# Moving dWq and WK2 blocks in the order of TensorE's work, and transposing Y and KV earlier, in the backward pass of a linear-attention and SwiGLU block

## The chip, the cores and the metric

The kernel runs on one core of a Trainium2 chip. The metric is the device time of one execution in microseconds; three runs of the kernel before gave 814.64, 814.79 and 814.91 us, so the median is 814.79 us.

Five engines work beside each other: TensorE (PE in the profile, with its weight loads as PEld) multiplies matrices into PSUM; VectorE (DVE), ScalarE (ACT) and GpSimd (POOL) do elementwise work; SyncE (SP) here only starts DMAs. In this kernel SP starts every transposing DMA, and POOL most of the plain loads and stores.

## The reference, cut to what matters

The block is a layer norm, linear attention with 32 heads of 20 columns, a residual, a second layer norm, a SwiGLU FFN and a second residual. The kernel returns the output and the gradients of the input and of the five weights, with S = 2048 rows, D = 640 and F = 1728, in bf16.

```python
def _A_ref(x, wqkv, wo):                      # x is the normalised input
    qkv = (x @ wqkv).reshape(B, S, 3, H, Dh).transpose(2, 0, 3, 1, 4)
    q, k, v = qkv[0], qkv[1], qkv[2]
    phi = lambda t: jnp.where(t > 0, t + 1, jnp.exp(t)) + 1e-6
    pq, pk = phi(q), phi(k)
    kv = jnp.einsum("bhsd,bhse->bhde", pk, v)
    z = jnp.einsum("bhsd->bhd", pk)
    num = jnp.einsum("bhqd,bhde->bhqe", pq, kv)
    den = jnp.einsum("bhqd,bhd->bhq", pq, z)[..., None] + 1e-6
    return (num / den).transpose(0, 2, 1, 3).reshape(B, S, D) @ wo
...
h = x + _A_ref(_layernorm(x), A_wqkv, A_wo)
h2 = h + _B_ref(_layernorm(h), B_w_gate, B_w_up, B_w_down)     # _B_ref: (silu(x@wg) * (x@wu)) @ wd
# outputs: h2, and the vjp of grad_out for x, wqkv, wo, w_gate, w_up, w_down
```

The kernel never forms v. It forms Y = xn^T pk (640x640) and from it, head by head, KV; in the backward pass it forms GT = dh1^T pqs and from it dKV. The names that this text uses: dWq and dWk are the gradients of the q and k parts of wqkv (`dwqk`), dWv that of the v part (`dwv`, from Y and dKV), dWo that of wo (`dwo`, from KV and G, the transpose of GT). WK2 is a 640x640 product of the v weights with dKV, and WV2 its transpose.

## The kernel before: the parts that the change touches

The program runs in this order: layer norm and k, q; Y and KV; the attention output; four FFN groups of 448 columns (384 in the last), each with its forward and backward products and weight gradients; the loop for dhn and dq; and the last third, with dk, dxn, and finally the FFN output `ps_o`.

Some parts of the program have their order fixed as written (`manual_schedule` names the engines); for the others the order of an engine's instructions is chosen when the program is built.

Y^T and KV^T are written to DRAM early:

```python
nc.sync.dma_start(out=mat_v(scr_Yt), in_=Yt)
...
nc.sync.dma_start(out=scr_KVT.rearrange("(j p) c -> p j c", p=P), in_=KVT)
```

In the FFN (SP's order is fixed, the others' is not) each pair of rows is transposed through one of three `stg` buffers to DRAM. The dwev tiles, which carry weight gradients out of PSUM, share six buffers with nsg, u and a:

```python
def stage():
    return small.tile([P, 7, P], BF16, name="stg", tag="stg", bufs=3)
...
fpool = wB.enter_context(tc.tile_pool(name="fpool", bufs=6))       # nsg, u, a, dwev
...
for g in range(4):
    for t in range(0, ST, 2):
        ...                                                        # pg, pu: matmuls into PSUM
        sig = nc.scalar.activation(out=dg, in_=pg[:, :, :w], func=ACT.Sigmoid)
        nc.scalar.activation(out=nsg, in_=pg[:, :, :w], func=ACT.Sigmoid, scale=-1.0)
        nc.scalar.copy(out=m, in_=pg[:, :, :w])
        nc.scalar.copy(out=u, in_=pu[:, :, :w])
        ...                                                        # seven products on DVE
        for c in range(2):
            stg = stage()
            nc.sync.dma_start_transpose(out=stg[:, :GK[g], :], in_=ddt[:, tt + c, 0:2 * w])
            nc.gpsimd.dma_start(out=scr_dT[t + c, :, KO[g]:KO[g] + GK[g], :], in_=stg[:, :GK[g], :])
    if g == 0:
        wdT = strips.tile([P, DT, 2 * GM], BF16, name="wdT", tag="S")
        load_wdT(wdT, 2)
    ...
    # then the weight gradients: eight dw() per group, each ending in
    ev = fw("dwev")
    last = copy(out=ev[:, :len(parts), :w], in_=ps[:, :len(parts), :w])
    for c, (_, _, dst) in enumerate(parts):
        nc.gpsimd.dma_start(out=dst[:, GO[g]:GO[g] + w], in_=ev[:, c, :w])
```

The last third, in which the order of SP and DVE is fixed. GT, woT and W2T lie in one tile, `mats`, and the later matrices take their places:

```python
W2T = mat(0, DT, D); woT = mat(DT * D, DT, D)                      # from the loop before
...
load_pk(0); load_pk(1)                                             # the first two pkr loads
...                                                                # SP: 16 transposes into wqkvT
GT = mat(2 * DT * D, DT, D)
for i in range(DT): ...                                            # ps_gt, copied by ACT into GT
dKVT = mat(0, HG, P)
KV = mat(HG * P, HG, P)
G = mat(2 * HG * P, HG, D)
Y = mat(2 * HG * P + HG * D, HG, D)
nc.gpsimd.dma_start(out=mat_v(scr_GT), in_=GT)
...
def load_pqT(v):                                                   # two transposes into ring
    nc.sync.dma_start_transpose(out=ring[:, 4 + v % 3], in_=scr_pk[v * P:(v + 1) * P, :])
    nc.sync.dma_start_transpose(out=ring[:, 7 + v % 3], in_=dq[v // 8][:, v % 8, :])

def wk2(i):
    ps = mm("ps_wk2")
    mm_heads(ps, lambda j: wqkvT[:, 10 + j, i * P:(i + 1) * P], lambda j, a, b: dKVT[:, j, a:b])
    nc.scalar.copy(out=half(WK2[:, i, :]), in_=row(ps))
    nc.sync.dma_start_transpose(out=WV2[:, :, i * P:(i + 1) * P], in_=WK2[:, i, :])

def dwqk(which, i):
    ev = wk("dwqk", pool=i % 2)
    ps = mm("ps_dwqk")                                             # 2 halves of 320 columns, 16 matmuls each
    ...
    nc.scalar.copy(out=half(ev[:]), in_=row(ps))
    nc.gpsimd.dma_start(out=out_2[i * P:(i + 1) * P, which * D:(which + 1) * D], in_=ev[:])

for v in range(3):
    load_pqT(v)
for t in range(ST):
    nc.vector.tensor_scalar(out=xn_r[:, t, :], ...)                # normalise x again
dz_add(ZL, ztmp)                                                   # two DVE operations each
kv_blocks(dKVT, "ps_dkvt", ...)                                    # dKV from woT and GT
for t in range(ZL + 1, ST):
    dz_add(t, ztmp)
...                                                                # dzs, two DVE operations
dwqk(0, 0)
for i in range(3):
    wk2(i)
dwqk(0, 1)
for i in range(3, DT):
    wk2(i)
dwqk(0, 2)
...                                                                # ps_dzb from dzs
for t in range(ST + LAG):                                          # LAG = 3
    if t in (2, 3):
        dwqk(0, t + 1)
    if t < ST:
        if t + 2 < ST:
            load_pk(t + 2)
        ...                                                        # ps_dk, then dk[:, t] on DVE
        nc.sync.dma_start_transpose(out=ring[:, t % 4], in_=dk[:, t, :])      # dkT
    if 8 <= t < 8 + HG:
        tr_cols(G[:, t - 8, :], scr_GT, OH[t - 8])
    if t == 14:
        nc.sync.dma_start_transpose(out=KV.rearrange("p j c -> p (j c)").unsqueeze(1), in_=scr_KVT)
    ...
    ps = mm("ps_dxn")                                              # u = t - 3: from dqT, pkT with WV2, dkT
    ...
for t in range(ST):                                                # the FFN output
    if t + MTA < ST:
        load_mT(t + MTA)                                           # a transpose into mT
    if t < 3:
        for j in (2 * t, 2 * t + 1):
            tr_cols(Y[:, j, :], scr_Yt, OH[j])
    if t + 3 < ST:
        load_h1(t + 3)                                             # a plain load into h1r
    ...                                                            # ps_o; dwo and dwv between
```

PSUM holds four of these tiles at a time.

Of the kernel before, what the change touches and what calls it, by code (L numbers as in the profile page):

```python
# [9 lines left out]
BF16 = mybir.dt.bfloat16  # L10
# [5 lines left out]
P = 128  # L16
# [4 lines left out]
def kernel(  # L21
# [67 lines left out]
    scr_dwdT = dram.tile([D, FT * P], BF16, name="scr_dwdT")  # L89
    scr_Yt = dram.tile([D, D], BF16, name="scr_Yt")  # L90
    scr_KVT = dram.tile([6 * P, P], BF16, name="scr_KVT")
    scr_GT = dram.tile([D, D], BF16, name="scr_GT")
    scr_W2T = dram.tile([D, D], BF16, name="scr_W2T")

# [10 lines left out]
    def mm_row(ps, lhs, rhs, n, start=True, stop=True):  # L105

        for ci in range(2):
            for k in range(n):
                nc.tensor.matmul(ps[:, ci, :320], lhsT=lhs(k), rhs=rhs(k, *NCH[ci]),  # L109
                                 start=(start and k == 0), stop=(stop and k == n - 1))  # L110
# [59 lines left out]
    def stage():  # L170
        return small.tile([P, 7, P], BF16, name="stg", tag="stg", bufs=3)
# [78 lines left out]
    def load_wdT(dst, g):  # L250
        o = GM if g == 1 else 0
        return nc.sync.dma_start_transpose(out=dst[:, :, o:o + GW[g]], in_=B_w_down[GO[g]:GO[g] + GW[g], :])
# [339 lines left out]
    with tc.manual_schedule(engines={EngineType.SP}):  # L592
# [14 lines left out]
        for g in range(4):  # L607
# [50 lines left out]
            if g == 0:  # L658
                wdT = strips.tile([P, DT, 2 * GM], BF16, name="wdT", tag="S")
                load_wdT(wdT, 2)  # L660
            elif g == 1:
                wgT[0] = big.tile([P, 14, D], BF16, name="wgT", tag="B")
                for gg in range(2):
                    tr_wgT(gg)
                    load_wgu(gg + 2)
            elif g == 2:
                dm_t[3] = strips.tile([P, ST, GM], BF16, name="dm3", tag="S")
                act_load(dm_t[3][:, :, :GW[3]], scr_dm_v)
                wgT[1] = big.tile([P, 13, D], BF16, name="wgT", tag="B")
                tr_wgT(2)  # L670
                tr_wgT(3)
            else:
                for c in range(4):
                    pool_store(scr_m_v[:, c * 4:(c + 1) * 4, F:FT * P], m_s[:, c * 4:(c + 1) * 4, w - 64:w])
                pool_store(mat_v(scr_dwdT)[:, 0:4, F:FT * P], zpad[:])
                pool_store(mat_v(scr_dwdT)[:, 4, F:FT * P], zpad[:, 0, :])
                load_cols(0, act_load)
# [40 lines left out]
    def dz_add(t, tmp):  # L718
        prod = tmp if t else zacc[:]
        nc.vector.tensor_tensor(out=hb(prod), in0=hb(pqs_tm[:, t, :]), in1=bc(nS1[:, t, :]), op=ALU.mult)  # L720
        if t:
            nc.vector.tensor_tensor(out=zacc[:], in0=zacc[:], in1=tmp, op=ALU.add)
# [85 lines left out]
    with tc.manual_schedule(engines={EngineType.SP, EngineType.DVE}):  # L808
# [13 lines left out]
        def tr_cols(dst, src, c):  # L822
            nc.sync.dma_start_transpose(out=dst.unsqueeze(1), in_=src[:, c:c + P])
# [39 lines left out]
            nc.scalar.copy(out=half(WK2[:, i, :]), in_=row(ps))  # L863
            nc.sync.dma_start_transpose(out=WV2[:, :, i * P:(i + 1) * P], in_=WK2[:, i, :])

        def dwqk(which, i):
            ev = wk("dwqk", pool=i % 2)
            ps = mm("ps_dwqk")
            mm_row(ps, lambda t: xn_r[:, t, i * P:(i + 1) * P],
                   lambda t, n0, n1: dq[t // 8][:, t % 8, n0:n1] if which == 0 else dk[:, t, n0:n1], ST)  # L870
            nc.scalar.copy(out=half(ev[:]), in_=row(ps))
            nc.gpsimd.dma_start(out=out_2[i * P:(i + 1) * P, which * D:(which + 1) * D], in_=ev[:])

# [3 lines left out]
            nc.vector.tensor_scalar(out=xn_r[:, t, :], in0=xn_r[:, t, :], scalar1=mv1[:, t, 0:1],  # L877
                                    scalar2=rstd1[:, t:t + 1], op0=ALU.subtract, op1=ALU.mult)
        ztmp = ring[:, 0:2].rearrange("p a k c -> p (a k c)").bitcast(FP32)
        dz_add(ZL, ztmp)  # L880
        kv_blocks(dKVT, "ps_dkvt", lambda i, a, b: woT[:, i, a:b], lambda i, a, b: GT[:, i, a:b])
        for t in range(ZL + 1, ST):
            dz_add(t, ztmp)
        dzs = [wk("dzs"), wk("dzl")]
        nc.vector.tensor_copy(out=dzs[0][:], in_=zacc[:])
        nc.vector.tensor_tensor(out=dzs[1][:], in0=zacc[:], in1=dzs[0][:], op=ALU.subtract)
        dwqk(0, 0)
        for i in range(3):
            wk2(i)
        dwqk(0, 1)  # L890
        for i in range(3, DT):
            wk2(i)
        dwqk(0, 2)
        ps = mm("ps_dzb")
        mm_row(ps, lambda k: ones[:], lambda k, n0, n1: dzs[k][:, n0:n1], 2)
        nc.scalar.copy(out=half(dzb[:]), in_=row(ps))
# [4 lines left out]
        def load_mT(t):  # L901
            if t % 4 == 0:
                mTs[t // 4] = strips.tile([P, 4, FT, P], BF16, name="mT", tag="S")
            nc.sync.dma_start_transpose(out=mTs[t // 4][:, t % 4], in_=scr_m[t * P:(t + 1) * P, :])

        for t in range(ST + LAG):
            if t in (2, 3):
                dwqk(0, t + 1)
# [3 lines that stand above are left out]
                pkr = pkrs.pop(t)  # L912
                nc.vector.tensor_scalar(out=pkr[:], in0=pkr[:], scalar1=-1e-6, scalar2=1.0, op0=ALU.add, op1=ALU.min)
                tk = wk("tk", pool=1)
                ps = mm("ps_dk")
                mm_row(ps, lambda i: xnT_r[:, t, i, :], lambda i, n0, n1: WK2[:, i, n0:n1], DT)
                nc.vector.scalar_tensor_tensor(out=half(tk[:]), in0=row(ps), scalar=rstd1[:, t:t + 1] if t < NC else 1.0,
                                               in1=half(dzb[:]), op0=ALU.mult, op1=ALU.add)
                nc.vector.tensor_tensor(out=dk[:, t, :], in0=tk[:], in1=pkr[:], op=ALU.mult)
                nc.sync.dma_start_transpose(out=ring[:, t % 4], in_=dk[:, t, :])  # L920
            if 8 <= t < 8 + HG:
                tr_cols(G[:, t - 8, :], scr_GT, OH[t - 8])
            if t == 14:
                nc.sync.dma_start_transpose(out=KV.rearrange("p j c -> p (j c)").unsqueeze(1), in_=scr_KVT)
            if t == ST:
                dKV = stage()[:, :HG, :]
                nc.sync.dma_start_transpose(out=dKV, in_=dKVT.rearrange("p j c -> p (j c)"))
            if t == ST:
                wd = big.tile([P, FT, D], BF16, name="wd", tag="B")
                nc.sync.dma_start(out=wd[:, :13, :], in_=B_w_down[0:13 * P, :].rearrange("(j p) d -> p j d", p=P))  # L930
                for r in (0, 64):
                    nc.sync.dma_start(out=wd[r:r + 64, 13, :], in_=B_w_down[13 * P:F, :])
            u = t - LAG
            if u < 0:
                continue
            if t >= ST:
                dwqk(1, t - ST)
            pkT, dqT, dkT = ring[:, 4 + u % 3], ring[:, 7 + u % 3], ring[:, u % 4]
            ps = mm("ps_dxn")
            for ci, (n0, n1) in enumerate(NCH):  # L940
                for k, (lhs, rhs) in enumerate(((dqT, wqkvT[:, 0:5]), (pkT, WV2), (dkT, wqkvT[:, 5:10]))):
                    for i in range(DT):
                        nc.tensor.matmul(ps[:, ci, :320], lhsT=lhs[:, i, :], rhs=rhs[:, i, n0:n1],  # L943
                                         start=(k == 0 and i == 0), stop=(k == 2 and i == DT - 1))
            if u + 3 < ST:
                load_pqT(u + 3)
            if ST - MTA <= u:
                load_mT(u - ST + MTA)
            dx = wk("dx")
            ln_bwd(ps, xn_r[:, u, :], rstd1[:, u:u + 1], dh1[:, u, :], dx[:], 0)  # L950
            nc.gpsimd.dma_start(out=o1_v[:, u, :], in_=dx[:])
# [60 lines left out]
        for t in range(ST):  # L1012
            if t + MTA < ST:
                load_mT(t + MTA)
            if t < 3:
                for j in (2 * t, 2 * t + 1):
                    tr_cols(Y[:, j, :], scr_Yt, OH[j])
            if t + 3 < ST:
                load_h1(t + 3)
            if t == ST - 1:  # L1020
                h1r = finish(t)
            late = t in (0, 1, 4, 5, 8, 9, 12, 14)
            for ci, (n0, n1) in enumerate(chunks(t)):
                for j in range(FT - 1):
                    part(t, ci, j, None, j == FT - 2 and not late)
                if t == ST - 1:
                    nc.vector.tensor_tensor(out=h1r[:, n0:n1], in0=po(t, ci), in1=h1r[:, n0:n1], op=ALU.add)
                    (nc.sync, nc.scalar, nc.sync)[ci].dma_start(out=o0_v[:, t, n0:n1], in_=h1r[:, n0:n1])
            if t in halves_at:
                n = 0  # L1030
                for u in halves_at[t]:
                    for ci in range(len(chunks(u))):
                        part(u, ci, FT - 1, n % 2, u <= t)
                        n += 1
                for u in halves_at[t]:
                    if u <= t:
                        finish(u)
            elif not late and t < ST - 1:
                finish(t)
            for f, i in small_of.get(t, ()):  # L1040
                f(i)
# [30 lines left out]
```

## Time and profile before

The profile is of one execution with a span of 814.1 us. The page gives busy times of the engines, the clock granted to TensorE in 40 slices, the chain of work that ended last, and groups of instructions; a group line gives source line, engine, operation, tiles, shapes and count, then busy time and mean, then the idle time of the engine ahead of it.

| what | us |
|---|---|
| median of three runs | 814.79 |
| TensorE busy / span of the profile | 808.3 / 814.1 |
| VectorE / ScalarE / GpSimd busy | 474.3 / 287.8 / 197.4 |
| first FFN group: first pg / first ps_dw / next group's first pg | 144.9 / 175.2 / 220.6 |
| end of ps_gt and start of ps_dkvt | 613.0 |
| first dxn | 644.4 |
| first ps_o | 747.7 |

TensorE's share of the chain that ended last is 96%. The queries used beside the page are the waits of one engine (who waited for whom, how long in total, how often, the longest), its timeline in a stretch of time (start, length, what, and in brackets the idle time before and who ended it), and, for one tile, the time from issue to landing of its DMAs.

### The profile page before, as it was taken

The page shows a single profiled execution, that of the slowest core. Times are in us where ns is not written, and L with a number is a line of the kernel's source. Part 1 is how long each engine was busy: PE and PEld are TensorE (multiplying, and loading weights), DVE is VectorE, ACT ScalarE, POOL GpSimd, SP SyncE. Part 2 cuts the span into 40 slices and gives each one's busy share as a digit, 9 for nine tenths or more (in the row PEclk, how much of TensorE's full clock was granted, in tenths as well). Part 3 has the DMA queues.
Part 4 walks back from the last instruction along what each step waited for, and adds up shares of the span by engine and source line. Part 5 has one row for each costly group of instructions (what it writes and reads, how often), then busy time and mean ns, then how long its engine had stood idle before and what let it go on. Part 6 is the DMA issues. An engine that isn't in the chain of part 4 may idle for free.

```text
span 814.1 us, 13869 instructions
## 1 busy us (share of the span) xinstructions
PE 808.3 (99%) x5476; PEld 519.9 (64%) x5476; DVE 474.3 (58%) x886; ACT 287.8 (35%) x405; POOL 197.4 (24%) x361
## 2 busy tenths in 40 slices
PE   8999999999999999999999999999999999999998
PEld 6776566555555555555666677777777777777676
DVE  7879988990096028800750158999897366631212
ACT  6972532760283035400831122322312133322010
POOL 4410045322422312221221711211220121112330
PEclk9999999999999999999999999999999999999999
DMA  9992799998669967994599677976499869999995
GB/s 303 178 344 79 171 180 292 233 263 199 192 147 220 236 154 170 194 267 78 125 148 191 226 232 215 217 209 170 114 242 165 164 131 167 166 237 205 194 237 134
DMA packets 276690, 158.49 MB, mean 195 GB/s; under 512 B 235005, under 2 KB 262782, under 8 KB 276625
## 3 DMA queue, kind: packets, MB, share of 16 engines
q1 hardware_dynamic: 251696, 82.12, 55.3%
q0 software_dynamic: 18416, 66.95, 27.2%
q10 hardware_dynamic: 6512, 8.54, 3.6%
q8 instruction: 43, 0.70, 0.4%
q14 instruction: 23, 0.18, 0.1%
HBM read 47.68 MB, written 53.66 MB: 124 GB/s over the span
## 4 chain that ended last, share of the span: by engine, by line
PE 96%; DMA 2%; DVE 1%; ACT 0%; POOL 0%; issue 0%; DVEq 0%
PE ps_dw L688 22%; PE ps_dhn L109 14%; PE ps_dxn L943 8%; PE pu L621 7%; PE pg L616 7%; PE ps_o L1001 6%; PE ps_kq L301 5%; PE ps_dm L391 5%; PE ps_dwqk L109 4%; PE ps_dp L109 3%; PE ps_gt L746 3%; PE ps_dk L109 3%; PE ps_y L488 3%; PE ps_a L546 3%; PE pdm L391 2%; DMA h1r<-scr_h 2%
## 5 line engine op out<-in xcount | busy, mean ns | idle before, releaser
L109 PE MATMUL ps_dhn<-wgT,cols 128*128 128x320 bf16 x864 | 119.5, 299 | 0.0
L688 PE MATMUL ps_dw<-dd,hn 128*128 128x448 bf16 (+1 forms) x640 | 118.8, 346 | 0.0
L109 PEld LDWEIGHTS <-cols 128*128 128x128 bf16 x864 | 84.5, 98 | 32.9
L688 PEld LDWEIGHTS <-hn 128*128 128x128 bf16 x640 | 62.6, 98 | 54.2
L690 DVE CAST dwev<-ps_dw 128x896 bf16<-128x896 f32 (+3 forms) x12 | 10.9, 908 | 136.6 <-PE ps_dw L688 111.6
L690 ACT CAST dwev<-ps_dw 128x896 bf16<-128x896 f32 (+1 forms) x20 | 17.6, 878 | 168.9 <-PE ps_dw L688 150.6
L653 POOL DMA_DIRECT2D scr_dT<-stg x64 | 34.6, 541 | 172.0 <-DMA stg<-dd 171.3
L621 PE MATMUL pu<-wgu,hnT 128*128 128x448 bf16 (+1 forms) x320 | 63.6, 346 | 0.0
L616 PE MATMUL pg<-wgu,hnT 128*128 128x448 bf16 (+1 forms) x320 | 63.6, 346 | 0.0
L1001 PE MATMUL ps_o<-wd,mT 128*128 128x320 bf16 (+3 forms) x462 | 61.1, 295 | 0.0
L688 PE MATMUL ps_dw<-m_s,dh 128*128 128x448 bf16 (+1 forms) x320 | 60.4, 346 | 0.0
L943 PEld LDWEIGHTS <-ring 128*128 128x128 bf16 x480 | 47.0, 98 | 18.2
L147 DVE CUSTOM_DVE_ANT_0 lb_a<-lb_dy,hn 128x640 bf16<-128x640 bf16 x32 | 26.4, 825 | 48.5 <-ACT lb_dy L145 48.5
L1001 PEld LDWEIGHTS <-mT 128*128 128x128 bf16 (+1 forms) x462 | 41.8, 97 | 17.5 <-issue 2.6
L943 PE MATMUL ps_dxn<-wqkvT,ring 128*128 128x320 bf16 x320 | 51.3, 299 | 0.0
L688 PEld LDWEIGHTS <-dh 128*128 128x128 bf16 x320 | 31.3, 98 | 27.1
L621 PEld LDWEIGHTS <-hnT 128*128 128x128 bf16 x320 | 31.3, 98 | 27.1
L616 PEld LDWEIGHTS <-hnT 128*128 128x128 bf16 x320 | 31.3, 98 | 27.0
L391 PEld LDWEIGHTS <-dh2T 128*128 128x128 bf16 x320 | 31.0, 98 | 25.1
L391 PE MATMUL ps_dm<-wdT,dh2T 128*128 128x448 bf16 (+1 forms) x240 | 46.5, 344 | 0.0
L301 PE MATMUL ps_kq<-wqk,xnT 128*128 128x320 bf16 x320 | 46.3, 299 | 0.2
L1008 DVE TENSOR_TENSOR h1r<-ps_o,h1r 128x640 bf16<-128x640 f32 x15 | 12.0, 822 | 53.2 <-PE ps_o L1001 37.6
(167 smaller groups left out, 1311.3 us busy)
## 6 DMA issues: line engine op xcount, KB each, us to landing
scr_dT<-stg POOLq DMA_DIRECT2D x48, 224.0 KB, 3.3
cols<-scr_dT POOLq DMA_DIRECT2D x6, 1728.0 KB, 9.1
scr_m<-m_s POOLq DMA_DIRECT2D x12, 448.0 KB, 4.6
cols<-scr_dT ACTq DMA_DIRECT2D x2, 1728.0 KB, 14.6
out_dram<-dwev POOLq DMA_DIRECT2D x30, 112.0 KB, 2.1
scr_dT<-stg POOLq DMA_DIRECT2D x16, 192.0 KB, 2.5
scr_pk<-pk SPq DMA_DIRECT2D x4, 640.0 KB, 8.1
scr_xnT<-xnT SPq DMA_DIRECT2D x4, 640.0 KB, 7.2
```

Source lines behind the costliest of these rows:

```text
L109: nc.tensor.matmul(ps[:, ci, :320], lhsT=lhs(k), rhs=rhs(k, *NCH[ci]), start=(start and k == 0), stop=(stop and k == n - 1))
L147: nc.vector.tensor_tensor_reduce(out=a[:], in0=dy[:], in1=xhat, scale=1.0, scalar=0.0, op0=ALU.mult, op1=ALU.add, accum_out=sums[:, 1:2])
L301: nc.tensor.matmul(ps[:, ci, :320], lhsT=xnT[:, t, k, :], rhs=wqk[:, k, w0 + n0:w0 + n1], start=(k == 0), stop=(k == DT - 1))
L391: nc.tensor.matmul(ps[:, c, :w], lhsT=dh2T[:, kt, (t + c) * P:(t + c + 1) * P], rhs=wdT[:, kt, o:o + w], start=(kt == 0), stop=(kt == DT - 1))
L488: nc.tensor.matmul(ps[:, ci, :320], lhsT=xn[:, t, i * P:(i + 1) * P], rhs=pk[:, t, n0:n1], start=(t == 0), stop=(t == ST - 1))
L616: nc.tensor.matmul(pg[:, c, :w], lhsT=hnT[:, kt, (t + c) * P:(t + c + 1) * P], rhs=wg[:, kt, 0:w], start=(kt == 0), stop=(kt == DT - 1))
L621: nc.tensor.matmul(pu[:, c, :w], lhsT=hnT[:, kt, (t + c) * P:(t + c + 1) * P], rhs=wg[:, kt, w:2 * w], start=(kt == 0), stop=(kt == DT - 1))
L653: nc.gpsimd.dma_start(out=scr_dT[t + c, :, KO[g]:KO[g] + GK[g], :], in_=stg[:, :GK[g], :])
L688: nc.tensor.matmul(ps[:, c, :w], lhsT=lhs(t), rhs=rhs(t), start=(t == 0), stop=(t == ST - 1))
L690: last = copy(out=ev[:, :len(parts), :w], in_=ps[:, :len(parts), :w])
L943: nc.tensor.matmul(ps[:, ci, :320], lhsT=lhs[:, i, :], rhs=rhs[:, i, n0:n1], start=(k == 0 and i == 0), stop=(k == 2 and i == DT - 1))
L1001: nc.tensor.matmul(po(t, ci), lhsT=mTs[t // 4][r, t % 4, j, :], rhs=wd[r, j, n0:n1], start=(t, ci) not in opened, stop=last)
```

## The change

It has two parts. In the last third, dWq block 0 is moved between GT and dKV, so that dKV does not follow directly on the copy of GT, and WK2 blocks 3 and 4 are put between the two halves of dWq block 2 (`between`). Two dz additions instead of one stand ahead of dKV.

The other part concerns Y and KV, which dWv and dWo need untransposed. Before, SP transposed them from scr_KVT and scr_Yt where they are used, KV at step 14 of the dk loop and Y at the beginning of the last stage. Now SP transposes them in the first FFN group, through the stg buffers; POOL stores them to two new DRAM tensors, and loads them in plain form at step YL = 5 of the dk loop. This takes seven transposes out of SP's queue in the last third, for seven transposes and seven stores in the FFN and two plain loads.

```diff
+    scr_Y = dram.tile([6 * P, D], BF16, name="scr_Y")
+    scr_KV = dram.tile([6 * P, P], BF16, name="scr_KV")
...
             if g == 0:
                 wdT = strips.tile([P, DT, 2 * GM], BF16, name="wdT", tag="S")
                 load_wdT(wdT, 2)
+                for j in range(HG):
+                    stg = stage()[:, :DT, :].rearrange("p k c -> p (k c)")
+                    nc.sync.dma_start_transpose(out=stg.unsqueeze(1), in_=scr_Yt[:, OH[j]:OH[j] + P])
+                    nc.gpsimd.dma_start(out=scr_Y[j * P:(j + 1) * P, :], in_=stg)
+                stg = stage()[:, :HG, :]
+                nc.sync.dma_start_transpose(out=stg.rearrange("p j c -> p (j c)").unsqueeze(1), in_=scr_KVT)
+                nc.gpsimd.dma_start(out=scr_KV.rearrange("(j p) c -> p j c", p=P), in_=stg)
...
-        def dwqk(which, i):
+        def dwqk(which, i, between=None):
             ev = wk("dwqk", pool=i % 2)
             ps = mm("ps_dwqk")
-            mm_row(ps, lambda t: xn_r[:, t, i * P:(i + 1) * P],
-                   lambda t, n0, n1: dq[t // 8][:, t % 8, n0:n1] if which == 0 else dk[:, t, n0:n1], ST)
+            for ci, (n0, n1) in enumerate(NCH):
+                for t in range(ST):
+                    nc.tensor.matmul(ps[:, ci, :320], lhsT=xn_r[:, t, i * P:(i + 1) * P],
+                                     rhs=dq[t // 8][:, t % 8, n0:n1] if which == 0 else dk[:, t, n0:n1],
+                                     start=(t == 0), stop=(t == ST - 1))
+                if between and ci == 0:
+                    between()
...
-        dz_add(ZL, ztmp)
+        for t in range(ZL, ZL + 2):
+            dz_add(t, ztmp)
+        dwqk(0, 0)
         kv_blocks(dKVT, "ps_dkvt", lambda i, a, b: woT[:, i, a:b], lambda i, a, b: GT[:, i, a:b])
-        for t in range(ZL + 1, ST):
+        for t in range(ZL + 2, ST):
             dz_add(t, ztmp)
         ...
-        dwqk(0, 0)
+        dwqk(0, 1)
         for i in range(3):
             wk2(i)
-        dwqk(0, 1)
-        for i in range(3, DT):
-            wk2(i)
-        dwqk(0, 2)
+        dwqk(0, 2, lambda: [wk2(i) for i in range(3, DT)])
...
+        YL = 5
...
-            if t == 14:
-                nc.sync.dma_start_transpose(out=KV.rearrange("p j c -> p (j c)").unsqueeze(1), in_=scr_KVT)
+            if t == YL:
+                nc.gpsimd.dma_start(out=Y[:], in_=scr_Y.rearrange("(j p) c -> p j c", p=P))
+                nc.gpsimd.dma_start(out=KV[:], in_=scr_KV.rearrange("(j p) c -> p j c", p=P))
...
-            if t < 3:
-                for j in (2 * t, 2 * t + 1):
-                    tr_cols(Y[:, j, :], scr_Yt, OH[j])
```

## The prediction, made before the changed kernel ran

> **What bounds the kernel now.** I read the page's busy row and clock row first, then TensorE's waits, then TensorE's timeline from 612 us, and last the issue times of SP (SyncE, which starts the transposing DMAs) and POOL (GpSimd, which starts the plain ones).
>
> ```profile
> PE 808.3 (99%) x5476; PEld 519.9 (64%) x5476; DVE 474.3 (58%) x886; ACT 287.8 (35%) x405; POOL 197.4 (24%) x361
> ...
> PEclk9999999999999999999999999999999999999999
> ```
>
> TensorE is busy for 808.3 of 814.1 us at full clock. The change alters no matmul, so all that it can give is part of the 5.8 us in which TensorE stands still; anything over that would have to be a new loss. TensorE's waits, longest first (us, times, longest):
>
> ```profile
> PE ps_warm L330 <- POOL ident masks.py:199: 1.6, 1, 1.6
> PE ps_t L285 <- DVE xn L274: 0.4, 1, 0.4
> PE ps_dwo L962 <- DVE h1r L1008: 0.4, 1, 0.4
> PE ps_dwqk L109 <- ACT wvk L863: 0.2, 1, 0.2
> PE ps_dkvt L509 <- ACT mats L843: 0.2, 1, 0.2
> ```
>
> The first two lie at the start and are untouched. The last two are what the reordering aims at; in the timeline they stand in brackets:
>
> ```profile
> 612.99 0.79 PE L509 MATMUL ps_dkvt<-mats 128*128 128x120 bf16 x12
> 613.93 0.96 PE L509 MATMUL ps_dkvt<-mats 128*128 128x120 bf16 x18 [0.15 <-ACT mats L843]
> 614.87 4.51 PE L109 MATMUL ps_dwqk<-dq,hn 128*128 128x320 bf16 x32
> 619.21 1.05 PE L128 MATMUL ps_wk<-mats,wqkvT 128*128 128x120 bf16 x21
> 620.46 4.51 PE L109 MATMUL ps_dwqk<-dq,hn 128*128 128x320 bf16 x32 [0.20 <-ACT wvk L863]
> ```
>
> The bracket leaves out the part of a wait that is covered by the modelled tail of the matmul before. Taken from start to start, against the usual distance of each kind of matmul, the same gaps are 0.32 us (inside dKV), 0.12 us (dKV to dWq) and 0.35 us (WK2 to dWq): 0.79 us together. The wait of dwo is 0.54 us in the same way of counting.
>
> [...] while POOL's four xnT_r loads (2.62 MB, issued at 591.7 to 594.7 us) are in flight, SP's transposes of a 160 KB piece are issued every 3.4 us and land after 10.4 us (median); after them the issues are mostly 1.28 us apart, landing after 4.7 us. [...] an uncontended dwev store of 112 KB lands in 2.1 us here[...].
>
> **The change, part one: the order of dWq, dKV and WK2.** dWq block 0 (32 matmuls, 4.35 us from start to start) moves between GT and dKV. By its end ACT has long copied the last GT row (0.69 us), so dKV waits for nothing: -0.32, and the 0.12 us after it should go too. Are its own inputs there? It would start at 612.99; the 16 normalised rows of xn_r are written by DVE until 613.03, and row t is needed only 0.136*t us after the start: no wait. dKV's mask products come after two dz additions on DVE instead of one (1.65 us more, done at about 616.2), while dKV now ends at about 619: no wait. The other four additions then start at about 619.5 and with dzs end at 627.5; dzb is wanted at about 629.0. That leaves 1.5 us of room. WK2 blocks 3 and 4 go between the halves of dWq block 2, so that ACT empties PSUM behind the first half; the wait of 0.35 us, all four PSUM buffers being held by one dWq and three WK2 tiles, should go because dWq block 1 is copied while WK2 runs. Sum: **-0.8 us**, all on the path.
>
> **Part two: six Y transposes and one of KV in the first FFN group.** SP runs late there. Its last stg transpose of the group is issued at 203.8 us, the wdT one at 205.65, and the next at 229.04, so there are 23 us free for seven pieces. A piece takes a stg buffer from its transpose to the landing of its store. Group 1 shows that cycle at rest: transpose at 229.04, landed 232.06, store at 232.59, landed 234.89, next use at 234.91, or 5.87 us for three buffers. So the pieces start at about 209.4, 211.9, 213.2, 215.3, 217.7, 219.0 and 221.1, and the KV store is issued at about 224.5. SP is free in time. The risk is POOL, which works its stores off in a fixed order:
>
> ```profile
> 207.31 0.54 POOL L653 DMA_DIRECT2D scr_dT<-stg  x1 [3.40 <-DMA stg<-dd]
> 207.84 0.54 POOL L692 DMA_DIRECT2D scr_dwdT<-dwev  x1
> 210.08 0.54 POOL L653 DMA_DIRECT2D scr_dT<-stg  x1 [1.70 <-DMA stg<-dd]
> 210.61 0.54 POOL L692 DMA_DIRECT2D scr_dwdT<-dwev  x1
> 211.14 2.13 POOL L692 DMA_DIRECT2D out_dram<-dwev  x4
> ```
>
> A dwev tile that DVE filled at 181 us is stored at 207.84 only, because the order was fixed by a plan in which the transposes run ahead. In the new order the Y stores will likely stand before the third or fourth pair of dwev stores, and these then go out after 224.5 instead of 212. dwev shares six buffers with nsg, u and a of the next group. nsg is due at 223.3 us, and TensorE notices a delay of ACT there after 3.1 us (the gate product is out of PSUM at 225.0, the buffer is wanted at 228.1). Third pair behind KV: stores until 226.1, landed 228.2, so nsg is 4.9 us late and TensorE loses 1.8. Third pair before KV: 0 to 0.2. I book **+0.4 us**.
>
> **Part three: the plain loads of Y and KV.** They replace one transpose at step 14 and six in the last stage, which cost SP 1.3 and some 14 us, but no wait of TensorE hangs on those: the only one there is dwo's, on an h1r load that lands 12.46 us after its issue among mT and Y transposes. SP will fill the gap with further mT transposes at once, so the DMA engines stay as full, and I book only **-0.1 us**. The loads themselves are 0.98 and 0.20 MB on POOL. The text puts them at step 5 of the dk loop, near 655 us, where they would be harmless: each dkT is fetched three steps ahead. But POOL is not held to program order here, and a load goes out as soon as its buffer is free. Three pkr loads, written in the same stretch after the dq loop, are issued in the middle of the last FFN group:
>
> ```profile
> 452.24 1.08 POOL L692 DMA_DIRECT2D scr_dwdT<-dwev  x2
> 453.36 1.07 POOL L818 DMA_DIRECT2D pkr<-scr_pk  x2
> ```
>
> Y lies on woT and GT, which are free when dKV has been computed and the GT store has landed (614.17 + 6.8 = 621.0 us); KV lies on W2T, free at 602. If they are moved up in that way, they fall into the one stretch in which SP is late:
>
> ```profile
> 591.94 16.18 SPq L823 DMA_TRANSPOSE wqkvT<-in_A_wqkv_dram  x6
> 608.16 16.86 SPq L728 DMA_TRANSPOSE wqkvT<-in_A_wqkv_dram  x10
> ...
> 633.13 7.35 SPq L864 DMA_TRANSPOSE wvk<-wvk  x5
> 640.57 6.62 SPq L920 DMA_TRANSPOSE ring<-dk  x4
> ```
>
> SP issues without a pause from 592 to 645 us, with the DMA engines' share at 0.88 to 1.10. The end of that row is what the first dxn needs: WV2's last piece (issued 638.39, landing after 4.0 us: 642.4) at 645.09, and the first dkT (640.57 + 3.7 = 644.3) at 645.77. With TensorE 0.8 us earlier the room is 1.9 and 0.65 us. What would the loads cost SP? From 591.94 to 605.54 four issues took 13.6 us, with the xnT_r loads and one hn load (0.66 MB, issued at 590.93) in flight: 13.6 - 4*1.3 = 8.4 us lost to 3.28 MB, or 2.6 us per MB, so 1.18 MB cost about 3.0 us. Less 0.65 of room, TensorE loses about 2.4 us; some of it may be taken up by the 12% of DMA time that is free from 622 to 634, so 2.0. I give the early issue three chances in four: **+1.5 us**.
>
> Sum: 814.8 - 0.8 + 0.4 - 0.1 + 1.5 = **815.8 us**.
>
> **The rivals.** (a) The loads stay at step 5 and the FFN stores slip in without harm: the waits of 0.79 us are gone and nothing comes in their place, 814.0. For it speaks that the program writes them at step 5, against it the pkr loads at 453 us. (b) The loads move up and SP becomes the bound before the first dxn: 816 to 817. (c) POOL's order in the FFN holds up the buffers of group 1: with (a) 815 to 816, with (b) 818. (d) With Y out of the last stage the DMA engines are quieter there and h1r lands early: dwo's 0.54 us go as well, at best 813.5. The landing of mT speaks against it: 30.4 us for the last eight pieces, one behind the other, so SP will only be finished sooner.
>
> **Range and chances.** The low end is (a) with (d): 813.4. The high end is (b) with (c) in their worse forms: 818.6. Both are within 0.5% of before; 2% would be 16 us, over five times the largest loss worked out here. Chances: faster 0.01, same 0.98, slower 0.01.
>
> **What would show it.** Part one is right if the two waits on ACT are gone and dzb starts at about 629.0. For part two look at ACT's first nsg of group 1 (223.3 before) and TensorE's third pg (228.1). For part three look at when POOL issues Y: near 621, with TensorE then waiting for ring or wvk at the first dxn, or near 655. If Y goes out near 621 and the first dxn does not wait, my cost per MB is wrong. If the time falls below 813.4, some wait was larger than these gaps show.

## The result, and the profile after

The changed kernel took 823.63 us in the median, against 814.89 for the kernel before: a ratio of 1.0118, with an interval of 1.0079 to 1.0158. It is slower by some 1.2%, and outside the predicted range of 813.4 to 818.6. Single executions of one kernel spread by several us here (821.3 to 830.6 for the changed kernel), for reasons that the traces below show only in part, so small differences of medians say little.

The profiled execution has a span of 820.8 us, 6.7 more than before. TensorE's waits of the changed kernel (us in total, times, longest):

```profile
PE pg L618 <- ACT m_s L644: 6.2, 1, 6.2
PE ps_warm L332 <- POOL ident masks.py:199: 1.6, 1, 1.6
PE ps_dw L697 <- DVE m_s L651: 0.2, 1, 0.2
```

The three short waits that the change and its side effects could remove (`ps_dwqk`, `ps_dkvt`, `ps_dwo`) are gone, and one of 6.2 us has come, beside one of 0.2. The long one lies in the second FFN group, far from the reordered part. Followed upstream, first in TensorE's timeline of the changed kernel:

```profile
226.06 2.06 PE L623 MATMUL pu<-wgu,hnT 128*128 128x448 bf16 x10
234.27 3.68 PE L618 MATMUL pg<-wgu,hnT 128*128 128x448 bf16 x10 [6.16 <-ACT m_s L644]
237.79 2.05 PE L623 MATMUL pu<-wgu,hnT 128*128 128x448 bf16 x10
```

then in ACT's:

```profile
222.94 0.92 ACT L639 ACTIVATE dd<-pg 128x896 bf16<-128x896 f32 x1
232.51 0.92 ACT L643 ACTIVATE nsg<-pg 128x896 bf16<-128x896 f32 x1 [8.64 <-DMA out_dram<-dwev]
233.32 0.90 ACT L644 CAST m_s<-pg 128x896 bf16<-128x896 f32 x1
```

and in POOL's, where 217.92 is the second pair of dwev stores and 229.77 the third:

```profile
217.39 0.54 POOL L666 DMA_DIRECT2D scr_Y<-stg  x1 [0.25 <-issue]
217.92 1.07 POOL L701 DMA_DIRECT2D out_dram<-dwev  x2
221.63 0.54 POOL L666 DMA_DIRECT2D scr_Y<-stg  x1 [2.64 <-DMA stg<-scr_Yt]
224.36 1.15 POOL L666 DMA_DIRECT2D scr_Y<-stg  x2 [2.19 <-DMA stg<-scr_Yt]
228.94 0.84 POOL L669 DMA_DIRECT2D scr_KV<-stg  x1 [3.43 <-DMA stg<-scr_KVT]
229.77 1.08 POOL L701 DMA_DIRECT2D out_dram<-dwev  x2
230.85 1.07 POOL L701 DMA_DIRECT2D scr_dwdT<-dwev  x2
```

The kernel before has, in the same two places:

```profile
223.31 0.91 ACT L641 ACTIVATE nsg<-pg 128x896 bf16<-128x896 f32 x1
227.97 2.05 PE L616 MATMUL pg<-wgu,hnT 128*128 128x448 bf16 x10
```

Read from the bottom: the third pair of dwev stores goes out at 229.77 only, behind the KV store, which waited for its own transpose. The pair lands at 232.41; nsg, which takes over the buffer, starts at 232.51 instead of 223.31; the copy of m, which frees the PSUM tile, follows; and TensorE's third pg starts at 234.27 instead of 227.97. The ten matmuls after the wait take 3.52 us from start to start of the next group instead of 1.89. The windows say why (PE, PEld, DVE, ACT and POOL busy, granted clock, DMA share, GB/s):

```profile
228.00:234.20 6.20, 0.12 (x1) 0.00 (x0) 0.00 (x0) 1.69 (x3) 5.26 (x10) 0.72 0.40 146
234.20:237.80 3.60, 3.53 (x11) 1.40 (x11) 3.51 (x7) 3.60 (x6) 1.44 (x3) 0.53 0.42 153
237.80:241.60 3.80, 3.80 (x22) 1.97 (x21) 3.77 (x8) 3.71 (x5) 0.00 (x0) 1.00 0.54 101
```

TensorE's clock was granted at half from 230.8 to 237.6 us (0.50 in that stretch, 1.00 in the 3.4 us before and after it): it fell 2.7 us after the end of TensorE's last matmul (228.12) and came back 3.3 us after the start of its next (234.27). What sets these two times this trace does not show; the last section puts the other executions beside it. The half clock makes the wait dearer by 1.6 us.

The last third looks as planned:

```profile
621.03 4.51 PE L880 MATMUL ps_dwqk<-dq,hn 128*128 128x320 bf16 x32
625.38 1.59 PE L511 MATMUL ps_dkvt<-mats 128*128 128x120 bf16 x30
626.82 4.51 PE L880 MATMUL ps_dwqk<-dq,hn 128*128 128x320 bf16 x32
631.16 1.05 PE L130 MATMUL ps_wk<-mats,wqkvT 128*128 128x120 bf16 x21
632.11 2.33 PE L880 MATMUL ps_dwqk<-dq,hn 128*128 128x320 bf16 x16
634.28 0.75 PE L130 MATMUL ps_wk<-mats,wqkvT 128*128 128x120 bf16 x14
```

No bracket is left between these. The account of the 6.7 us, from start to start of matmuls: +6.3 for the wait at pg, +1.6 for the half clock, +0.4 for two gaps in the weight gradients that follow, -0.3 for a gap at ps_dp that the change doesn't touch, -0.8 for the waits in the last third, -0.5 for dwo's. The wait of ps_t at the very start, which is gone as well, gives nothing: the warm-up matmuls ahead of it took 0.5 us longer.

### The profile page after: what moved, and what is told of

Its sections match the earlier page's. It is cut to its first block, busy times and chain, and to the rows that moved or that the text cites. A ratio compares the mean times of both kernels' runs of the same rounds, so it can differ in the third digit from the quotient of the medians.

```text
span 820.8 us, 13901 instructions
## 1 busy us (share of the span) xinstructions
PE 810.0 (99%) x5476; PEld 520.7 (63%) x5476; DVE 474.0 (58%) x886; ACT 288.0 (35%) x405; POOL 203.1 (25%) x370
## 4 chain that ended last, share of the span: by engine, by line
PE 92%; DVE 3%; DMA 3%; issue 1%; SPq 0%; ACT 0%; POOL 0%; POOLq 0%; DVEq 0%; ACTq 0%
PE ps_dw L697 19%; PE ps_dhn L111 14%; PE ps_dxn L958 8%; PE ps_o L1016 7%; PE ps_kq L303 5%; PE ps_dwqk L880 5%; PE ps_dm L393 5%; PE pu L623 5%; PE pg L618 5%; PE ps_dk L111 3%; PE ps_dp L111 3%; PE ps_y L490 3%; PE ps_gt L755 3%; PE ps_a L548 3%; PE pdm L393 2%; DMA stg<-scr_Yt 1%
## 5 line engine op out<-in xcount | busy, mean ns | idle before, releaser
L618 PE MATMUL pg<-wgu,hnT 128*128 128x448 bf16 (+1 forms) x320 | 65.3, 352 | 6.2 <-ACT m_s L644 6.2
L651 DVE TENSOR_TENSOR m_s<-m_s,dd 128x896 bf16<-128x896 bf16 (+1 forms) x32 | 19.3, 604 | 42.8 <-ACT m_s L644 42.8
```

The costliest lines, as they stand in the source:

```text
L618: nc.tensor.matmul(pg[:, c, :w], lhsT=hnT[:, kt, (t + c) * P:(t + c + 1) * P], rhs=wg[:, kt, 0:w], start=(kt == 0), stop=(kt == DT - 1))
```

## The experiments

The theory: in the first FFN group the stores of Y and KV stand in POOL's fixed order ahead of the third pair of dwev stores; these hold buffers that ACT needs in the second group. Rivals: the reordering costs something itself; the additional transposes, the stg buffers or the DMA traffic hold up the second group; the early plain loads stop the first dxn.

### The order alone, and the move alone

`e1_order_only` keeps the new order of dWq, dKV and WK2; Y and KV are transposed late, as before.

```diff
-                for j in range(HG): ...            # Y and KV through stg, in the FFN
-            if t == YL: ...                        # their plain loads
+            if t == 14:
+                nc.sync.dma_start_transpose(out=KV..., in_=scr_KVT)
...
+            if t < 3:
+                for j in (2 * t, 2 * t + 1):
+                    tr_cols(Y[:, j, :], scr_Yt, OH[j])
```

> Only the new order of dWq, dKV and WK2 in the last third; Y and KV are transposed late as before. Theory (the loss lies in the FFN, where POOL's stores of Y and KV stand ahead of the dwev stores and hold the six buffers): both short waits on ACT go, 814.1 us, 0.8 below the kernel before. Rival (the reordering costs something of its own in the last third): above 815.5.

815.37 us, ratio 1.0008 (0.9986 to 1.0029). No cost of the reordering shows; whether it gains can't be told from this ratio. The lowest execution, 813.96, is 0.8 below the lowest of before beside it, 814.74; but three of its 12 executions took over 823 us, of before one of 29. The profiled execution was one of the long ones, and its wait lies in the last stage, on a transposed tile of mT:

```profile
PE ps_o L1008 <- DMA mT<-scr_m: 8.3, 2, 8.1
```

That mT piece took 21.3 us from issue to landing. The kernel before should be open to this wait as well, since there too Y is transposed among the mT tiles; no such execution of it was profiled.

`e2_ffn_only` is the opposite: Y and KV moved, the order of before.

```diff
-        def dwqk(which, i, between=None):
+        def dwqk(which, i):
...
-        dwqk(0, 2, lambda: [wk2(i) for i in range(3, DT)])
+        ...                                        # as in the kernel before
```

> Only the move of Y and KV; the order in the last third as before. Theory: the whole loss is here, 822 to 824 us, with one wait of TensorE of about 6 us at the third pg of the second FFN group and slower matmuls after it. Rival (the reordering has a share in the loss): below 819.

825.64 us, ratio 1.0126 (1.0092 to 1.016). The loss is all here. Its waits show both at once, the new one and one of those that the reordering would have removed:

```profile
PE pg L618 <- ACT m_s L644: 11.0, 1, 11.0
...
PE ps_dwqk L111 <- ACT wvk L872: 0.2, 1, 0.2
```

### POOL's order, taken away in two ways

`e3_sp_stores` lets SP issue the seven stores. The transposes, buffers and bytes stay; only POOL's order is without them.

```diff
-                    nc.gpsimd.dma_start(out=scr_Y[j * P:(j + 1) * P, :], in_=stg)
+                    nc.sync.dma_start(out=scr_Y[j * P:(j + 1) * P, :], in_=stg)   # two transposes later
```

> As changed, but SP instead of POOL issues the seven stores of Y and KV, each two transposes behind its own; the transposes, the three stg buffers and the bytes are the same. Theory (POOL's order): the dwev stores are no longer behind them, the wait at pg goes, 813.5 to 814.3 us. Rival (the transposes, the stg buffers or the DMA traffic themselves hold up the second group): 820 or more.

815.48 us, ratio 0.9995 (0.9974 to 1.0015); the profiled execution took 814.94 and has one wait left. The waits, then POOL's second and third pair of dwev stores, then SP's timeline in the first two groups:

```profile
PE ps_warm L332 <- POOL ident masks.py:199: 1.6, 1, 1.6
```

```profile
211.03 2.13 POOL L716 DMA_DIRECT2D out_dram<-dwev  x4
```

```profile
209.52 6.62 SPq L667 DMA_TRANSPOSE stg<-scr_Yt  x3
...
233.99 0.37 SPq L677 DMA_DIRECT2D scr_KV<-stg  x1
234.46 3.93 SPq L654 DMA_TRANSPOSE stg<-dd  x3
```

The third dwev pair goes out at 212.1, as in the kernel before (212.2), and not at 229.77. The KV store goes out at 233.99, even later than in the changed kernel, and the second group's first transpose at 234.46 (229.04 in the kernel before), and TensorE doesn't notice either. So it is neither the transposes nor the stg buffers nor SP's lateness. The median is still above the expected range of 813.5 to 814.3; some of its executions took 816 to 823 us, and only one of the 18 was profiled, so the waits of the others aren't seen.

`e6_dwev_first` leaves the stores with POOL, but behind all dwev stores of the group.

```diff
             dw([dgu_part(i, 0), dgu_part(i, 1)], nc.scalar.copy)
+            if g == 0:
+                for j in range(HG): ...            # transposes as before, stores by pool_store (order kept)
```

> As changed, but the seven pieces are written behind the weight gradients of the first group, and their stores on POOL keep that order, so every dwev store goes ahead of every Y store. Theory (POOL's order): no wait at pg or pu, 813.5 to 815.5 us; SP's first stg transpose of the second group comes up to 8 us later, which nothing on TensorE's path feels. Rival (the stg buffers or SP's lateness hold up the second group): a wait in the second group or at the start of the third, 818 or more.

815.93 us, ratio 1.0004 (0.9988 to 1.0019): the wait at pg is gone, with the dwev stores early again. The median is a little above the expected 813.5 to 815.5. The profiled execution, one of the longer ones with 818.75 us, shows a wait that I had predicted and not found in the changed kernel's profile, at the first dxn:

```profile
210.96 2.13 POOL L694 DMA_DIRECT2D out_dram<-dwev  x4
```

```profile
PE ps_dxn L960 <- DMA ring<-dk: 3.5, 1, 3.5
```

### The buffer, and the length of the chain

`e5_bufs7` keeps POOL's order and gives dwev, nsg, u and a one buffer more.

```diff
-    fpool = wB.enter_context(tc.tile_pool(name="fpool", bufs=6))
+    fpool = wB.enter_context(tc.tile_pool(name="fpool", bufs=7))
```

> As changed, but with seven buffers instead of six for dwev, nsg, u and a; POOL's order stays. By the rotation of the buffers nsg then takes the one of the second dwev pair, stored ahead of the last Y pieces, and u the one of the third, behind KV. Theory (a buffer held by a late dwev store is what stops ACT): nsg runs about on time, u is what waits, and TensorE's wait moves from the third pg to the third pu and shortens by about 2 us; 1.5 to 3 us below the changed kernel in the same call. Rival (the lateness of POOL's stores hurts in another way, not by the buffers): no difference from the changed kernel.

823.58 us, ratio 1.0086 (1.0067 to 1.0105), beside 825.31 for the changed kernel: 1.7 less, at the low end of what was expected, and within the spread of both. The profile tells more. ACT's timeline:

```profile
224.50 0.92 ACT L643 ACTIVATE nsg<-pg 128x896 bf16<-128x896 f32 x1 [1.45 <-DMA out_dram<-dwev]
225.32 0.90 ACT L644 CAST m_s<-pg 128x896 bf16<-128x896 f32 x1
236.77 0.91 ACT L645 CAST u<-pu 128x896 bf16<-128x896 f32 x1 [10.55 <-DMA out_dram<-dwev]
```

nsg runs about on time and u waits instead, as the rotation of seven buffers has it; TensorE's wait has moved from pg to pu. The buffer is the link. The wait is not shorter in this execution, 8.1 us instead of 6.2, because the stores came later (first Y transpose at 214.12, see the table below).

`e4_kv_late` takes one piece, KV, out of the seven.

```diff
-                nc.sync.dma_start_transpose(out=stg..., in_=scr_KVT)
-                nc.gpsimd.dma_start(out=scr_KV..., in_=stg)
```

> As changed, but KV stays as before (one late transpose), so six pieces in the FFN instead of seven. Theory (POOL's order): the third pair of dwev stores follows the sixth Y store, issued near 225.0, and lands near 228.4; TensorE may be late by 226.4 without loss, so it waits about 2 us and the clock stays full: 815.5 to 816.5 us. Rival (a loss in proportion to the pieces): six sevenths of it stay, 821 to 822.

822.24 us, ratio 1.0087 (1.006 to 1.0114): a miss, far above 815.5 to 816.5, and near the rival's figure. `e8_after_again` is the changed kernel once more.

> The changed kernel once more, on the same chip as the others of this call. Theory: a wait of TensorE at the third pg that follows SP's time: about 22 us pass from the first Y transpose to the landing of the third dwev pair, so that each us by which SP starts Y later lengthens the wait by one; 821 to 828 us. Rival (the wait is of fixed length and the spread is from elsewhere): the same 6.2 us of wait whenever Y starts.

825.31 us, ratio 1.0114 (1.0076 to 1.0153). Set side by side, the five profiles show what was wrong with the expectation for KV. Times are from issues and landings in each trace, in us from the span's start:

| kernel | first Y transpose issued | third dwev pair landed | between | wait of TensorE |
|---|---|---|---|---|
| changed | 210.28 | 232.41 | 22.1 | 6.2 at pg |
| e8_after_again | 211.54 | 233.20 | 21.7 | 6.2 at pg |
| e2_ffn_only | 215.31 | 237.73 | 22.4 | 11.0 at pg |
| e5_bufs7 | 214.12 | 236.67 | 22.6 | 8.1 at pu |
| e4_kv_late (six pieces) | 215.34 | 233.31 | 18.0 | 4.2 at pg, 1.3 at pu |

Seven pieces take some 22 us, six take 18: the chain has the structure that the theory gives it, and without KV it is 4 us shorter. But its start moves between 210 and 215 us from execution to execution, since SP reaches the first Y transpose when it is through with its backlog of the first group (in the changed kernel the wdT transpose ahead of it keeps SP until 210.18). A later start makes the wait longer: in e2 the start is 5.0 us later than in the changed kernel and the wait 4.8 longer. For e4 I had taken the start of the profile at hand, 210.3, as fixed, and I had left out the half clock, 2.5 us in that execution by an estimate from its windows (clock 0.50 from 235 to 238 us and 0.63 from there to 241, half of the time at half clock taken as lost); it also waited 1.4 us for dh, which the change doesn't touch. By its time alone e4 speaks for its rival; what speaks against it is this one trace. The rival of a fixed wait falls with e2; e8 alone would not have told, as its TensorE came 0.7 us later as well.

### The plain loads

`e7_pinned` is e3 with the loads of Y and KV held at step 5 of the dk loop, where the program text has them.

```diff
-                nc.gpsimd.dma_start(out=Y[:], in_=scr_Y...)
+                tc.keep_in_program_order(nc.gpsimd.dma_start(out=Y[:], in_=scr_Y...))     # KV alike
```

> As the version whose Y and KV stores are issued by SP, but the plain loads of Y and KV are kept at step 5 of the dk loop. Theory (the early issue costs SP about 2 us, which the room before the first dxn takes up): no difference from that version in the time, within 0.5 us; SP's chain before the first dxn is about 2 us shorter. Rival (the early loads cost TensorE time in some executions): lower by 1 us or more in the median.

819.39 us, ratio 1.0053 (1.0038 to 1.0068), in all four executions between 818.95 and 820.89: worse than the early loads. My theory falls here. TensorE's timeline, and the windows at that place:

```profile
663.94 1.52 PE L111 MATMUL ps_dk<-wvk,xnT_r 128*128 128x320 bf16 x10
668.67 1.36 PE L973 MATMUL ps_dxn<-wqkvT,ring 128*128 128x320 bf16 x5 [3.20 <-DMA ring<-dq]
```

```profile
660.00:665.30 5.30, 5.30 (x41) 3.72 (x38) 3.31 (x9) 1.80 (x3) 1.08 (x2) 1.00 1.03 171
665.30:668.60 3.30, 0.17 (x2) 0.00 (x0) 1.31 (x4) 0.92 (x1) 0.00 (x0) 1.00 1.17 148
668.60:672.00 3.40, 3.33 (x14) 1.92 (x15) 1.95 (x4) 0.00 (x0) 1.08 (x2) 0.54 1.26 211
```

The dqT transpose issued at 656.35, just after the Y load (655.98), lands 12.3 us later (the sixteen dqT transposes of the kernel before took 2.7 to 6.1 us, median 3.5), and is wanted sooner. The clock behind the wait was 0.54 for 3.4 us, which by the same kind of estimate is 1.6 us more, 4.8 us in all.

`e9_split_loads` is e3 with Y brought back in six pieces.

```diff
-            if t == YL: ...
+            if YL <= t < YL + HG:
+                pool_store(Y[:, t - YL, :], scr_Y[(t - YL) * P:(t - YL + 1) * P, :])      # order kept
+            if t == YL + HG:
+                pool_store(KV[:], scr_KV.rearrange("(j p) c -> p j c", p=P))
```

> As the version whose Y and KV stores are issued by SP, but Y comes back in six loads of 160 KB at steps 5 to 10 of the dk loop and KV at step 11, each held in its place. Theory (a load of 1 MB at once slows SP's transposes for some 6 us; small ones spread over steps of 5.4 us do not): no wait at any dxn, 813.5 to 814.3 us in an execution without other waits, below the kernel before by 0.5 to 1.3 us. Rival (any such load in the dk loop takes the room that SP has there): waits at dxn, 815.5 or more.

`e10_order_again` ran beside it.

> Once more the new order alone, with Y and KV transposed late, beside the version above. Theory (its gain is the two waits of 0.8 us, its outliers come from late mT transposes in the last stage, where Y is still transposed): 814.0 to 814.8 us with some executions above 820. Rival (no gain at all): 814.9 to 815.3 us.

e9: 814.69 us, ratio 1.0007 (0.9991 to 1.0024). e10: 814.60 us, ratio 0.9989 (0.9965 to 1.0012). The kernel before had 815.32 beside them. e10 lies in its expected range; e9 is 0.4 above its own, and its profiled execution took 814.72 without a wait but the one at the very start. In e9's profile no dxn waits, and the pieces land after 4.0 to 6.4 us; the ring transposes beside them take 4.6 us to land (median), as long as in e10, which has no such loads. The lowest executions are 814.15 and 814.10 against 814.63 of before, 0.5 less, in the direction of the two removed waits; by the intervals neither version is shown to beat the kernel before. The last mT tile lands at 783.5 us in e9's profile and at 801.4 in that of before, but at 789.8 in e10's, where Y is still transposed among the mT tiles, so single profiles don't tell what the move of Y gives there. Whether it makes long executions rarer is open: e9 had one of 14 above 820, e10 one of 14, before two of 27.

## Why the prediction was wrong

**The order (part one): right.** The waits of 0.79 us went (0.74 from start to start), without a new one; dzb starts 16.0 us after the first dWq block, as worked out.

**The FFN stores (part two): the step that failed, by size.** The prediction named the mechanism, the buffer and the place: "Third pair behind KV: ... nsg is 4.9 us late and TensorE loses 1.8." Then it booked +0.4, leaning towards the milder order. It was the harsher one, and it cost 7.9 us in the profiled execution (6.3 of wait, 1.6 of half clock). Its terms were too small:
- KV's store went out at 228.94, not "at about 224.5". The first transpose came 0.9 us later than assumed. Three buffers took 7.0 and 7.4 us for a round, not 5.87, a figure taken where the DMA share was 0.63 (229 to 235 us of the kernel before); here it was 1.02 from 210 to 215 us and 0.67 to 0.73 from there to 229, with transposes, Y stores and dwev stores in flight, and a Y transpose took 3.1 to 5.2 us to land instead of 3.0. That makes 3.6 us, and KV's own transpose and store another 0.8.
- So nsg was 9.2 us late instead of 4.9. The 3.1 us of room was right: 9.2 - 3.1 = 6.1, measured 6.2.
- The half clock that came with the wait, 1.6 us here and 2.9 in e5 (an estimate from the windows in the last section), was not in the sum at all.
- The start of the chain was taken as fixed; in other executions it lies up to 5 us later. The median is 1.1 us above the profiled execution; a later start or a longer half clock would do that, but the other executions weren't profiled.

**The plain loads (part three): mechanism right, size off in either direction, and one claim wrong.** They did move up: Y was issued at 627.87, which is 619.9 by the clock of before (TensorE was 8.0 us later), and 621.0 was predicted. SP's six ring transposes took 10.3 us instead of 8.1, so 2.2 us were lost, a little under the 3.0 of the estimate; and no dxn waited in that execution, but in e6 the same six took 15.4 us and TensorE waited 3.5. Of the seven profiled executions with the early load, e6's alone waited; in e3 the first dkT landed 0.3 us before it was wanted. The +1.5 lies between these outcomes, which doesn't make it their mean. That the loads would be "harmless" at step 5 was wrong: the prediction looked at dkT, which is fetched three steps ahead, and in e7 TensorE waits 3.2 us for dqT, whose landing took 12.3 us beside the load, against 2.7 to 6.1 in the kernel before.

**dwo's wait:** gone as well, but in e10 too, in which Y stays in the last stage, and in e2, in which the order stays; so it is owed to neither alone, and the kernel before may lack it in other executions.

## What to carry to other kernels

On an engine that issues DMAs in a fixed order, a store that waits for a slow transfer holds up the unrelated stores behind it (here KV's store waited 3.4 us for its transpose, and the third dwev pair behind it went out at 229.77 instead of 212.2); before adding one, ask which buffers those others hold and who takes them over next. Work such a chain out with landing times from a stretch as busy as the one that it will run in, and with the spread of its start. The half clock belongs in the sum as well: in these profiles seven of the eight waits of TensorE of 3.2 us or more were made dearer by 1.6 to 2.9 us (mostly estimates, in the table below); beside the eighth (3.5 us, e6) the mean clock stayed at 1.00. Here a load of 1 MB that was split over six steps left the transposes beside it alone (4.6 us to land in e9, as in e10 without it); the same load at once didn't, neither early (six ring transposes took 15.4 us in e6, 8.1 in the kernel before) nor at step 5 (12.3 us to land for one of them in e7).

## What the runs showed of the hardware that I had not expected

A wait of 3.2 us (e7) was enough for half clock, while with one of 3.5 us in e6 the mean clock of the whole execution stayed at 1.00. The eight waits of TensorE of over 3 us, with the clock granted in the windows around the end of each (us of each trace):

| execution | wait | granted clock | at half clock | TensorE later by |
|---|---|---|---|---|
| e7_pinned | 3.2 | 1.00 in 665.3 to 668.6, 0.54 to 672 | at least 3.1 | 1.6 |
| e6_dwev_first | 3.5 | 1.00 in the mean of the execution | none seen | none seen |
| e4_kv_late | 4.2 | 0.80 in 231 to 235, 0.50 to 238, 0.63 to 241 | 6.8 | 2.5 |
| changed | 6.2 | 0.50 in 230.8 to 237.6 | 6.8 | 1.6 |
| e8_after_again | 6.2 | 0.89 in 228.5 to 234.8, 0.50 to 238.4, 0.74 to 242 | 6.9 | 2.6 |
| e5_bufs7 | 8.1 | 0.74 in 229.5 to 237.6, 0.50 to 241, 0.68 to 245 | 10.2 | 2.9 |
| e1_order_only | 8.1 | 0.80 in 798 to 806.4, 0.52 to 810, 1.00 to 814 | 6.8 | 1.7 |
| e2_ffn_only | 11.0 | 0.73 in 228 to 239.3, 0.50 to 242.9, 0.92 to 246.6 | 10.3 | 2.0 |

The last two columns are estimates, but for the changed kernel's: in the one, what a window's mean lacks of 1.00, doubled; in the other, half of the part of that which lies in TensorE's work behind the wait. The length of the wait does not settle the time at half clock: two waits of 6.2 us went with 6.8 and 6.9 us of it, but two of 8.1 us with 6.8 and 10.2, and of the two shortest one went with it and one without. What does settle it, these profiles do not show.

The dqT transpose (160 KB) that was issued 0.4 us after a plain load of 0.98 MB, with KV's of 0.20 MB behind that, took 12.3 us to land (e7), against 2.7 to 6.1 us in the kernel before. The load itself landed after 7.4 us in the changed kernel and after 12.1 us in e6.
